# Row maxima over 256 and 512 keys instead of 384 and 384, with a mask copy, a sign step and two sums in other places

## The chip, the cores and the metric

The kernel runs on one core of one Trainium2 chip. The metric is the device time of one execution in microseconds (us). Five engines work side by side, each through its own queue in order: TensorE (PE, matrix products), VectorE (DVE), ScalarE (ACT), GpSimd (POOL) and SyncE (SP, which issues most DMAs). They wait for each other through semaphores. A matrix product reads its operands from the on-chip memory SBUF and leaves its result in PSUM, of which the tiles named `wide`, `sc` and `turned` are parts.

## What is computed

Routing attention and then a feed-forward layer with a gate. Cut to what matters:

```python
# q, k, v: (4, 8, 768, 64); centroids: (8, 16, 64)
q_assign = argmax(q_n . c_n); k_assign = argmax(k_n . c_n)     # nearest of 16 clusters
mask = q_assign[..., :, None] == k_assign[..., None, :]
scores = where(mask, (q @ k.T) / 8, -1e9)
scores = scores - max(scores, axis=-1)
attn = exp(scores); attn = attn / (sum(attn) + 1e-9)
x = attn @ v                                                   # then (3072, 512)
h = x @ w_in                                                   # (3072, 2048)
out = (h * erf(softplus(h))) @ w_out                           # (3072, 512)
```

## The kernel before

The kernel has an attention stage of about 400 us and a feed-forward stage of about 550 us. The diff touches the first.

A *pair* is two heads of one batch entry; there are 16 pairs (0 to 15), each with its two heads in rows 0 to 63 and 64 to 127. A pair is worked in 12 *units*: `units[u]` is a pair, a half of its 768 queries (384) and a block of 128 keys. Two units make a *period*, so `period(p, i)` with i from 0 to 5 is called 96 times, and i = 0, 1, 2 belong to the first half of the queries and i = 3, 4, 5 to the second. All instructions are kept in the order in which the program writes them, per engine: the wrapper `InOrder` records them, which is why nearly every row of the profile has its line, L131.

A row's maximum must be known before its exponentials. So half a pair ahead, `maxima_step` computes a bound on the scores of one block of 128 queries in bfloat16: two passes of matrix products into `wide` (`qv` times `kv`, the values; `qm` times `km`, the cluster masks), one product for each head, and then a DVE reduction of `wide` into `nmx`. There is one `wide`. A block's 768 keys are taken in two such steps of 384 keys, so a period has two: the *first step* (`step_ahead(u)`) with both passes on 64 rows, and the *second step* (`step_ahead(u + 1, True)`), which is a generator: its first pass stands alone, and its second pass uses only rows 32 to 63 and 96 to 127, beside the score products on rows 0 to 31 and 64 to 95. With every third block (periods 2 and 5) a small reduction into `lowest` follows, and `turn` brings the bounds into a row of `qm` in the next period.

In a period PE does, in this order: in periods 0 and 3 `turn`; the first step; `products` of units u and u + 1 (float32, into two `sc` buffers that are reused every two units); the first pass of the second step; `scores(u)` with the second pass of the second step beside it; `scores(u + 1)`; in some periods a product for a mask of the next pair, into `turned`; in period 3 `similarities` of the pair after the next one; `attend` for the two units before (float32, into `turned`); and in periods 0 and 3 the first product of `divide`, which sums the denominators.

DVE's queue has the two reductions, and between them: in periods 1 and 4 the three operations of `divide` (`den`, two on `turned`, one into `more_out`); the cluster choice of `choose`, in period 3 as `sims`, a maximum that is stored in a corner of the `sc` buffer of unit u + 1, and `hot`, in period 5 `aside`, in period 0 `hotT`; transposes of q and k; and, in period 0, one mask copy into `km` (`masks`, with `copied_by` set to DVE).

ACT has the exponentials (`curve(u)`, `curve(u + 1)`) that read `sc` and write one of eight tiles `pr`, the logarithm and exponential of `divide`, and the other mask copies.

POOL sums the exponentials: `accumulate` adds each unit's `pr` to a running sum in `more_out`. Its first sum of each half takes the first two units at once, in periods 1 and 4.

Beside this, in pairs 1 to 11, 22 of the 32 blocks of the feed-forward weights are converted, two blocks a pair. A block (`n`) goes through `size` and `rest` (ACT), `bounded` and `shifted` (DVE, each 128x512 from SBUF to SBUF, the first float32 and the second uint32), `sign` (ACT, from 128x512 to int16) and `summed` (POOL, which needs `sign` and `shifted`), after which SP issues the `fetch` of the block five later. For one block of a pair, `n1 - 1`, `bounded`, `shifted` and `sign` are in period 0 and `summed` in period 1; for the other, `n1`, `bounded`, `sign` and `shifted` are in period 3 and `summed` in period 4. In pairs 12 to 15 (`FORMS`) some sums of the weights take the place.

Of the kernel before, what the change touches and what calls it, by code (L numbers as in the profile page):

```python
# [14 lines left out]
ALU = mybir.AluOpType  # L15
ACT = mybir.ActivationFunctionType
AX = mybir.AxisListType
PSUM = bass.MemoryType.PSUM

P = 128  # L20
B, H, S, D = 4, 8, 768, 64
C = 16
NJ = S // P
# [15 lines left out]

UP = 2.0**16  # L40
PLACES = 5
FORMS = {12: {0: 1}, 13: {0: 1}, 14: {0: 1, 3: 1}, 15: {0: 1, 3: 2, 4: 2, 5: 2}}
POOL_FORMS = range(12, 16)
BIG = 2.0**60
# [95 lines left out]
def kernel(  # L140
# [178 lines left out]
    def sign(n):  # L319
        hi, _, upper = steps[n]  # L320
        turned_sign = n < 4 * DM // P and n // (DM // P) % 2 == 0
        ae.activation(
            out=upper, in_=hi, func=ACT.Prelu, scale=-(2.0**-25) if turned_sign else 2.0**-25, alpha=2.0**90
        )
# [78 lines left out]
    def choose(p, spare=None, aside=False):  # L403

        if p >= NPAIR:
            return
        st = pairs[p]
        n = HW // C
        sims = routep.tile([P, HW], F32, name="sims")
        ve.transpose(out=sims, in_=st.pop("psim"))  # L410
        yield
        sim = sims.rearrange("p (g c) -> p g c", c=C)
        mx = (wide[:, 0] if spare is None else spare)[:, 512 - n :]
        ve.reduce_max(out=mx, in_=sim, axis=AX.X)
        yield
        hot = routep.tile([P, HW], BF16, name="hot")
        ve.tensor_tensor(
            out=hot.rearrange("p (g c) -> p g c", c=C), in0=sim,
            in1=mx.unsqueeze(2).to_broadcast([P, n, C]), op=ALU.is_equal,
        )  # L420
        yield
        if aside:
            st["aside"] = routep.tile([P, HW], BF16, name="aside")
            ve.transpose(out=st["aside"][D + Q :], in_=hot[D : D + Q])
            yield
        st["hotT"] = routep.tile([P, HW], BF16, name="hotT")
        ve.transpose(out=st["hotT"], in_=hot)
# [5 lines left out]
    def masks(p, nm, half, bank, narrow=False, copied_by=ae):  # L433

        if p >= NPAIR:
            return lambda: None
        st = pairs[p]
        cols = slice(half * HW, (half + 1) * HW)
        r, hot = slice(0, D) if nm == "q" else slice(D, P), st["hotT"]
        picked = pick[r, half]  # L440
        if narrow:
            r = slice(r.start + Q, r.stop)
            picked = pick[r, 1]
            hot = hot if half else st["aside"]
        won = bank[:, 0:HW]
        te.matmul(won, lhsT=picked, rhs=hot[r], start=True, stop=True)
        if nm == "q":
            return lambda: ae.activation(out=st["qm"][:, cols], in_=won, func=ACT.Relu)
        if copied_by is ve:
            return lambda: ve.tensor_scalar(  # L450
                out=st["km"][:, cols], in0=won, scalar1=BIG, scalar2=nbig, op0=ALU.mult, op1=ALU.add
            )
        return lambda: ae.activation(
            out=st["km"][:, cols], in_=won, func=ACT.Identity, bias=nbig, scale=BIG
        )

    turns = []

    def maxima_step(p, i, sm=wide, behind=False):

        st = pairs[p]
        nmx = maxima[p % 2]
        t, half = divmod(i, 2)

        def passes(a, b, start, rows):
            for e in range(2):
                r = slice(e * D + rows.start, e * D + rows.stop)
                te.matmul(
                    sm[:, e, 0:HW], lhsT=st[a][r, t * P : (t + 1) * P],
                    rhs=st[b][r, half * HW : (half + 1) * HW], start=start, stop=not start,  # L470
                )

        passes("qv", "kv", True, slice(0, D))
        if behind:
            yield
        passes("qm", "km", False, slice(Q, D) if behind else slice(0, D))
        if behind:
            yield
        ve.tensor_reduce(
            out=nmx[:, :, t, half], in_=sm[:, :, 0:HW], axis=AX.X, op=ALU.max, negate=True  # L480
        )
        if i in (NJ - 1, 2 * NJ - 1):
            h = i // NJ
            ve.tensor_reduce(
                out=lowest[h][:, :, ::D].rearrange("p t e -> p e t"),
                in_=nmx[:, :, h * HJ : (h + 1) * HJ], axis=AX.X, op=ALU.min,
            )
            turns.append((p, h))
# [48 lines left out]
    def curve(u):  # L537

        pr = prs[u % NPT]
        sc = sc_of.pop(u)[:, :, 0:HW].rearrange("p e (c x) -> p e c x", c=2)  # L540
        ae.activation(out=pr[:, :, :, 0:QW], in_=sc, func=ACT.Exp, scale=D**-0.5)
# [801 lines left out]

    def step_ahead(u, behind=False):
        p, i = divmod(u + NJ, 2 * NJ)
        steps = maxima_step(p, i, behind=behind) if p < NPAIR else iter(())
        if not behind:
            run(steps)
        return steps
# [7 lines left out]
    def period(p, i):  # L1357
        u = 2 * NJ * p + 2 * i
        n1, n2 = 2 * p - 1, 2 * p
        early = lambda n: 0 <= n < N_EARLY  # L1360

        def mask(place):
            which = (MASKS if p else FIRST_MASKS).get((i, place))
            if which:
                return masks(p + 1, *which, turned[0 if i in (0, 5) else 1], place > 1, ve if i == 0 else ae)
            return lambda: None

        if u > 0:
            for which in turns if i in (0, 3) else ():
                turn(*which)  # L1370
                turns.remove(which)
            step_ahead(u)
        mask(0)()
        next(part[0], None)
        if i == 5:
            next(routing[0], None)
        if i == 0 and p:
            run(routing[0])
        if u == 2:
            next(routing[0])  # L1380
        products(u)
        products(u + 1)
        mask(1)()
        second = step_ahead(u + 1, True) if u > 0 else iter(())
        next(second, None)
        rows = D if u == 0 or u + NJ >= len(units) else Q
        scores(u, rows)
        next(second, None)
        if i:
            next(second, None)  # L1390
        next(part[0], None)
        scores(u + 1, rows)
        later = mask(2)
        if i == 0:
            later()
            later = lambda: None
            next(second, None)
        if i == 3:
            similarities(p + 2)
            routing[0] = choose(p + 2, sc_of[u + 1][:, 0], True)  # L1400
        curve(u)
        later()
        curve(u + 1)
        if u == 0:
            step_ahead(1)
            similarities(1)
            routing[0] = choose(1, turned[0])
            next(routing[0])
            next(routing[0])
            vectors(1, "q")  # L1410
            vectors(1, "k")
        if i == 0 and early(n1 - 1):
            bounded(n1 - 1)
            shifted(n1 - 1)
            sign(n1 - 1)
        elif i == 1 and early(n1):
            size_and_rest(n1)
        elif i == 3 and early(n1):
            bounded(n1)
            sign(n1)  # L1420
        elif i == 5 and early(n2):
            rest(n2)
        for _ in range(min(len(forms), FORMS.get(p, {}).get(i, 0))):
            forms.pop(0)[0]()
        if i == 3:
            next(routing[0], None)
            if early(n1):
                shifted(n1)
            for _ in range(2):
                next(routing[0], None)  # L1430
        elif i == 1:
            load(p + 1, "v", v, vp)
            if p == 0:
                run(routing[0])
                transposes(2, "q")
        elif i == 2:
            transposes(p + 2, "k")
        elif i == 4:
            vectors(p + 2, "k")
            vectors(p + 2, "q")  # L1440
        elif i == 5:
            transposes(p + 3, "q")
        if u > 0:
            if i == 1 and early(n1 - 1):
                summed(n1 - 1)
            elif i == 4 and early(n1):
                summed(n1)
            for w in (u - 2, u - 1):
                accumulate(w)
            if i % HJ == 1 and p in POOL_FORMS and forms:  # L1450
                forms.pop(0)[1]()
            for w in (u - 2, u - 1):
                attend(w)
            if i % HJ == 0:
                part[0] = divide(u - 1)
                next(part[0])
        if i == 3 and early(n2):
            size(n2)

# [185 lines left out]
```

## Time and profile before

| | |
|---|---|
| median of 3 runs | 964.01 us (963.83 to 964.29) |
| the profiled execution | 963.98 us |
| its span, from the first instruction to the last | 962.2 us |
| mean granted clock of TensorE | 1.00 |

The costliest groups of the attention stage, from the fifth part of the page (line, engine, operation, output and inputs with partitions x elements, count, then busy time in all and mean ns of one, then the engine's idle time ahead of them):

```profile
L131 POOL TENSOR_TENSOR more_out<-more_out,pr 128x768 f32<-128x768 f32 x128 | 217.1, 1696 | 18.5 <-ACT pr L131 10.0
L131 DVE TENSOR_REDUCE nmx<-wide 128x2 f32<-128x768 f32 x189 | 180.5, 955 | 47.8 <-PE wide L131 47.0
L131 ACT ACTIVATE pr<-sc 128x768 f32<-128x768 f32 x192 | 148.7, 810 | 94.3 <-PE wide L131 78.7
L131 PE MATMUL turned<-pr,in_v 128*32 128x193 f32 x3072 | 144.8, 330 | 0.0
```

A timeline row has the start and the length in us from the span's start, the engine, the operation, its output and inputs, the shapes, how many of them follow each other, and in brackets how long the engine was idle before and what ended that. A length is from the start of the first to the end of the last of the row; on DVE and ACT an operation is shown to begin up to a tenth of a us or more before the one ahead of it has ended, and on PE several products run at once. A row of windows has, for each stretch, its length and the busy time of PE, weight loads, DVE, ACT and POOL with the number of instructions, then the granted clock, the DMA share and GB/s. A row of the chain of waits has a start, a length and what the end waited for in that time.

### The profile page before, as it was taken

The page shows a single profiled execution, that of the slowest core. Times are in us where ns is not written, and L with a number is a line of the kernel's source. Part 1 is how long each engine was busy: PE and PEld are TensorE (multiplying, and loading weights), DVE is VectorE, ACT ScalarE, POOL GpSimd, SP SyncE. Part 2 cuts the span into 40 slices and gives each one's busy share as a digit, 9 for nine tenths or more (in the row PEclk, how much of TensorE's full clock was granted, in tenths as well). Part 3 has the DMA queues.
Part 4 walks back from the last instruction along what each step waited for, and adds up shares of the span by engine and source line. Part 5 has one row for each costly group of instructions (what it writes and reads, how often), then busy time and mean ns, then how long its engine had stood idle before and what let it go on. Part 6 is the DMA issues. An engine that isn't in the chain of part 4 may idle for free.

```text
span 962.2 us, 22508 instructions
## 1 busy us (share of the span) xinstructions
PE 953.1 (99%) x8954; PEld 729.3 (76%) x8954; DVE 772.0 (80%) x1336; ACT 550.2 (57%) x839; POOL 544.7 (57%) x385
## 2 busy tenths in 40 slices
PE   8999999999999999999999999999999999999998
PEld 3555555555555555588888888998999899889987
DVE  8888888888888887878879878488847966795787
ACT  3777777777777665557624442564258226724651
POOL 1688888778787888835789902650353054206500
PEclk9999999999999999999999999999999999999999
DMA  9444444446444311282994349653564538254423
GB/s 214 83 112 111 111 111 109 107 110 174 89 111 111 68 35 35 67 276 66 182 206 192 144 168 233 215 183 118 189 201 129 166 135 260 75 186 156 152 88 110
DMA packets 180921, 134.42 MB, mean 140 GB/s; under 512 B 131888, under 2 KB 141616, under 8 KB 180784
## 3 DMA queue, kind: packets, MB, share of 16 engines
q1 hardware_dynamic: 173600, 123.37, 44.2%
q0 software_dynamic: 4720, 9.18, 5.4%
q8 instruction: 71, 1.16, 0.5%
q10 hardware_dynamic: 2496, 0.43, 0.2%
q14 instruction: 34, 0.28, 0.1%
HBM read 99.39 MB, written 35.39 MB: 140 GB/s over the span
## 4 chain that ended last, share of the span: by engine, by line
PE 95%; DVE 2%; POOL 1%; DMA 1%; issue 1%; ACT 0%; SPq 0%; DVEq 0%; POOLq 0%; ACTq 0%
PE bank L131 42%; PE turned L131 31%; PE sc L131 16%; PE wide L131 6%; POOL more_out L131 1%; DVE nmx L131 1%; DMA g_more<-in_moe_w_out_dram 0%; DMA in_q<-in_q_dram 0%; DVE kT L131 0%; DVE turned L131 0%; DVE sims L131 0%; POOL x_more L131 0%; DVE qT L131 0%; DVE more_out L131 0%; ACT pr L131 0%
## 5 line engine op out<-in xcount | busy, mean ns | idle before, releaser
L131 POOL TENSOR_TENSOR more_out<-more_out,pr 128x768 f32<-128x768 f32 x128 | 217.1, 1696 | 18.5 <-ACT pr L131 10.0
L131 DVE TENSOR_REDUCE nmx<-wide 128x2 f32<-128x768 f32 x189 | 180.5, 955 | 47.8 <-PE wide L131 47.0
L131 ACT ACTIVATE pr<-sc 128x768 f32<-128x768 f32 x192 | 148.7, 810 | 94.3 <-PE wide L131 78.7
L131 PE MATMUL turned<-pr,in_v 128*32 128x193 f32 x3072 | 144.8, 330 | 0.0
L131 PEld LDWEIGHTS turned<-pr,in_v 128*32 128x32 f32 x3072 | 91.5, 109 | 50.7 <-issue 21.3
L131 DVE TENSOR_TENSOR g<-g,bank 128x512 f32<-128x512 f32 (+1 forms) x139 | 77.9, 578 | 50.1 <-PE bank L131 44.2
L131 PE MATMUL bank<-x_own,w_in 128*128 128x128 f32 (+1 forms) x712 | 106.6, 296 | 0.0
L131 POOL TENSOR_TENSOR x_own<-x_own 128x512 f32<-128x512 f32 x16 | 23.0, 1448 | 146.7 <-DVE x_own L131 133.9
L131 PE MATMUL sc<-qT,kT 64*128 64x384 f32 x528 | 98.3, 486 | 0.0
L131 PEld LDWEIGHTS bank<-x_own,w_in 128*128 128x128 f32 x712 | 94.2, 192 | 4.7 <-DVE g L131 0.8
L131 DVE TENSOR_TENSOR g<-g 128x512 f32<-128x512 f32 x114 | 79.0, 693 | 20.0 <-PE bank L131 14.2
L131 POOL TENSOR_TENSOR g<-g,osb 128x512 f32<-128x512 f32 x40 | 51.9, 1310 | 48.5 <-DVE g L131 35.5
L131 PE MATMUL bank<-w_out,g 128*128 128x256 f32 x336 | 77.0, 379 | 0.0
L131 POOL TENSOR_TENSOR more_out<-pr,pr 128x768 f32<-128x768 f32 x32 | 60.4, 1887 | 28.3 <-ACT pr L131 28.3
L131 PEld LDWEIGHTS bank<-w_out,g 128*128 128x128 f32 x336 | 63.7, 190 | 9.0 <-DVE g L131 0.3
L131 PE MATMUL bank<-g_more,g 128*128 128x256 f32 x288 | 68.3, 380 | 0.0
L131 PEld LDWEIGHTS <-qv 64*128 64x128 bf16 x384 | 27.0, 93 | 53.0 <-issue 36.9
L131 PEld LDWEIGHTS sc<-qT,kT 64*128 64x128 f32 x528 | 50.0, 187 | 21.3 <-ACT inv L131 2.4
L131 PE MATMUL wide<-kv,qv 64*128 64x384 bf16 x378 | 64.1, 328 | 1.3 <-DVE nmx L131 0.6
L131 PE MATMUL wide<-km,qm 64*128 64x384 bf16 (+1 forms) x378 | 62.6, 327 | 0.0
L131 DVE TENSOR_TENSOR g<-a_s,g 128x512 f32<-128x512 f32 x64 | 59.8, 971 | 3.1 <-ACT a_s L131 3.1
L131 ACT ACT_TABLE_LOAD x40 | 51.3, 1283 | 18.5 <-DVE g L131 17.9
(215 smaller groups left out, 1994.8 us busy)
## 6 DMA issues: line engine op xcount, KB each, us to landing
g_more<-b_dram SPq DMA_DIRECT2D x48, 512.0 KB, 3.3
w_in<-a_dram SPq DMA_DIRECT2D x64, 256.0 KB, 3.4
more_in<-a_dram SPq DMA_DIRECT2D x48, 256.0 KB, 3.5
x_own<-in_moe_w_in_dram SPq DMA_DIRECT2D x13, 512.0 KB, 4.4
in_v<-in_v_dram SPq DMA_DIRECT2D x32, 192.0 KB, 3.0
x_dram<-more_out SPq DMA_DIRECT2D x128, 48.0 KB, 1.8
x_own<-x_dram SPq DMA_DIRECT2D x6, 1024.0 KB, 5.9
in_k<-in_k_dram SPq DMA_DIRECT2D x59, 96.0 KB, 2.7
```

Of the source, the lines that this page charges most:

```text
L131: ins = getattr(self.engine, name)(*args, **kw)
```

## The change

Four edits, and what moves with them:

1. `maxima_step` takes `cut`, the key at which the two steps divide. From unit 12 on (pair 1), in periods 0, 1, 3 and 4, the first step takes 256 keys and the second 512. In periods 2 and 5, and before unit 12, it stays 384 and 384.
2. The mask copy of period 0 moves from DVE to ACT, for all pairs that have it (the masks of pairs 2 to 15, in pairs 1 to 14), and it stands behind the second step's reduction in the program and ahead of `curve(u)` on ACT. The moved `later()` changes nothing in other periods.
3. `sign(n1 - 1)` of period 0 moves behind the first product, the logarithm and the exponential of `divide`.
4. `accumulate` of the two units before now stands ahead of `summed`, in period 1 and in period 4.
5. With `summed` moves the `fetch` behind it; nothing else changes its order.

```diff
+NARROW = 2 * P
...
-    def maxima_step(p, i, sm=wide, behind=False):
+    def maxima_step(p, i, sm=wide, behind=False, cut=HW):
...
+        keys = slice(cut, S) if half else slice(0, cut)
+        width = keys.stop - keys.start
...
-                    sm[:, e, 0:HW], lhsT=st[a][r, t * P : (t + 1) * P],
-                    rhs=st[b][r, half * HW : (half + 1) * HW], start=start, stop=not start,
+                    sm[:, e, 0:width], lhsT=st[a][r, t * P : (t + 1) * P],
+                    rhs=st[b][r, keys], start=start, stop=not start,
...
-            out=nmx[:, :, t, half], in_=sm[:, :, 0:HW], axis=AX.X, op=ALU.max, negate=True
+            out=nmx[:, :, t, half], in_=sm[:, :, 0:width], axis=AX.X, op=ALU.max, negate=True
...
     def step_ahead(u, behind=False):
         p, i = divmod(u + NJ, 2 * NJ)
-        steps = maxima_step(p, i, behind=behind) if p < NPAIR else iter(())
+        cut = NARROW if u >= 2 * NJ and u // 2 % HJ < HJ - 1 else HW
+        steps = maxima_step(p, i, behind=behind, cut=cut) if p < NPAIR else iter(())
...
-                return masks(p + 1, *which, turned[0 if i in (0, 5) else 1], place > 1, ve if i == 0 else ae)
+                return masks(p + 1, *which, turned[0 if i in (0, 5) else 1], place > 1)
...
         later = mask(2)
         if i == 0:
-            later()
-            later = lambda: None
             next(second, None)
         if i == 3:
             similarities(p + 2)
             routing[0] = choose(p + 2, sc_of[u + 1][:, 0], True)
+        if i == 0:
+            later()
+            later = lambda: None
         curve(u)
         later()
         curve(u + 1)
...
         if i == 0 and early(n1 - 1):
             bounded(n1 - 1)
             shifted(n1 - 1)
-            sign(n1 - 1)
...
         if u > 0:
+            for w in (u - 2, u - 1):
+                accumulate(w)
             if i == 1 and early(n1 - 1):
                 summed(n1 - 1)
             elif i == 4 and early(n1):
                 summed(n1)
-            for w in (u - 2, u - 1):
-                accumulate(w)
...
             if i % HJ == 0:
                 part[0] = divide(u - 1)
                 next(part[0])
+        if i == 0 and early(n1 - 1):
+            sign(n1 - 1)
```

## The prediction

> **What bounds the kernel now.** I read the first and fourth parts of the page, then the attention stage pair by pair, since the diff touches nothing else.
>
> ```profile
> span 962.2 us, 22508 instructions
> PE 953.1 (99%) x8954; PEld 729.3 (76%) x8954; DVE 772.0 (80%) x1336; ACT 550.2 (57%) x839; POOL 544.7 (57%) x385
> PE 95%; DVE 2%; POOL 1%; DMA 1%; issue 1%; ACT 0%; SPq 0%; DVEq 0%; POOLq 0%; ACTq 0%
> ```
>
> TensorE (PE) is busy 99% of the span and is 95% of the chain that ended last, so time moves only with PE's own work or with a new hole in it. Six consecutive periods (pair 7, from 190.10 us) are one turn of the loop:
>
> ```profile
> 202.14:206.80 4.66, 4.66 (x70) 2.47 (x70) 3.81 (x7) 3.48 (x6) 3.17 (x2) 1.00 0.52 84
> sum 24.44, PE 24.44 PEld 13.90 DVE 21.02 ACT 19.15 POOL 19.63; mean PE 4.07 PEld 2.32 DVE 3.50 ACT 3.19 POOL 3.27
> ```
>
> In these windows PE fills all 24.44 us of a pair at granted clock 1.00, with VectorE (DVE) 21.02 behind it. The chain of waits shows where DVE already touches PE:
>
> ```profile
> 195.98 0.19 PE wide L131 x2
> 203.86 0.16 PE wide L131 x2
> 208.61 0.20 PE wide L131 x2
> ```
>
> These are the first pass of the second maxima step in periods 1, 3 and 4. It must wait until DVE has reduced the first step out of the same tile `wide`. Period 3 does not wait (0.16). Periods 1 and 4 pay 0.03 and 0.04, of which I count 0.02 for period 1. So there DVE is already exactly as late as PE can bear.
>
> **The narrow and wide steps on PE.**
>
> ```profile
> 210.62 0.34 PE L131 MATMUL wide<-kv,qv 64*128 64x384 bf16 x2
> 210.79 0.33 PE L131 MATMUL wide<-km,qm 64*128 64x384 bf16 x2
> 210.95 1.45 PE L131 MATMUL sc<-qT,kT 64*128 64x384 f32 x8
> ```
>
> From start to start a pass over 384 keys takes 0.17 and 0.16 us; 128 keys are 0.053. The first step has two passes with nothing beside them: 256 keys save 0.107, of which I count 0.10, since the next weights must load meanwhile. The second step's first pass is alone too: 512 keys add 0.053. Its second pass uses 32-row strips that the score matmuls leave free. Whether the longer strip holds up the other strips, this view answers:
>
> ```profile
> 320.65 0.32 PE L131 MATMUL turned<-hotT,pick 64*128 64x384 bf16 x1
> 320.65 1.61 PE L131 MATMUL sc<-qT,kT 64*128 64x384 f32 x8
> ```
>
> The mask copy occupies rows 0 to 63 from 320.65; a score matmul starts on the other rows at the same 320.65 and the two halves then run staggered. Row strips run on their own, so I take 0 for that pass (bounds: 0, and 0.053 if strips march together), but in period 0 the narrow mask matmul stands behind it in its strip: 0.05. PE's balance is -0.05 in periods 1, 3 and 4, and 0 in period 0. Pairs 1 to 14 have all four narrow periods, pair 15 periods 0 (without mask) and 1.
>
> **DVE: same total, other places.** Reductions go from two of 768 numbers to 512 and 1024. Between 768 numbers (0.96) and 384 (0.55, below) lies 1.07 ns a number, so the first is 0.27 shorter and the second 0.27 longer. This is the queue of period 3:
>
> ```profile
> 204.40 0.96 DVE L131 TENSOR_REDUCE nmx<-wide 128x2 f32<-128x768 f32 x1 [0.83 <-PE wide L131]
> 204.41 1.51 ACT L131 ACTIVATE pr<-sc 128x768 f32<-128x768 f32 x2 [1.15 <-PE wide L131]
> 205.27 0.42 DVE L131 TENSOR_SCALAR w_in<-w_in 128x512 f32<-128x512 f32 x1
> 205.60 0.58 DVE L131 STREAM_TRANSPOSE sims<-turned 128x384 f32<-128x384 f32 x1
> 206.10 0.39 DVE L131 TENSOR_SCALAR w_in<-w_in 128x512 uint32<-128x512 uint32 x1
> 206.41 0.55 DVE L131 TENSOR_REDUCE sc<-sims 128x24 f32<-128x384 f32 x1
> 206.99 0.55 DVE L131 TENSOR_TENSOR hot<-sims,sc 128x384 bf16<-128x384 f32 x1
> 207.46 0.95 DVE L131 TENSOR_REDUCE nmx<-wide 128x2 f32<-128x768 f32 x1
> 208.47 0.34 PE L131 MATMUL wide<-kv,qv 64*128 64x384 bf16 x2
> 207.26 1.29 POOL L131 TENSOR_TENSOR w_in<-w_in,x_own 128x512 int32<-128x512 int32 x1 [1.87 <-ACT x_own L131]
> 208.51 1.85 POOL L131 TENSOR_TENSOR more_out<-pr,pr 128x768 f32<-128x768 f32 x1
> ```
>
> DVE runs without a hole from 204.40 to period 4's first reduction. Its start is bound to the end of period 3's second step: -0.10 +0.05 +0.05 on PE, so unmoved. The 0.27 added at its head and saved at its tail cancel. So in pairs 1 to 11 PE's savings of periods 3 and 4 are swallowed at period 4's second step, whatever else happens, and only its 0.05 longer pass remains.
>
> **The order on GpSimd (POOL), the term that decides.** Look at POOL above: it sits idle 1.87 us, until the sign step on ScalarE (ACT) ends, with `summed` at the head of its queue. In that hole lie both DVE operations on `w_in` (`bounded`, 205.27; `shifted`, 206.10). The edit puts the accumulations ahead of `summed` in periods 1 and 4, so POOL no longer waits for the sign but only for the two exponentials. The first accumulation's start then shows in pair 12, which has no `summed`:
>
> ```profile
> 326.75 1.51 ACT L131 ACTIVATE pr<-sc 128x768 f32<-128x768 f32 x2 [1.15 <-PE wide L131]
> 328.34 1.83 POOL L131 TENSOR_TENSOR more_out<-pr,pr 128x768 f32<-128x768 f32 x1 [1.14 <-ACT pr L131]
> 328.40 0.56 DVE L131 TENSOR_REDUCE sc<-sims 128x24 f32<-128x384 f32 x1
> ```
>
> It starts 0.08 after the exponentials end and lasts 1.83. In pair 7 that is 204.41 + 1.51 + 0.08 = 206.00, to 207.83. `shifted` would start at 206.10 + 0.27 = 206.37, inside it. What POOL does to such an operation stands in the stage after the attention:
>
> ```profile
> 441.04 1.28 POOL L131 TENSOR_TENSOR more_out<-more_out,w_out 128x512 f32<-128x512 f32 x1
> 441.31 1.30 DVE L131 TENSOR_SCALAR w_out<-w_out 128x512 f32<-128x512 f32 x1 [0.86 <-ACT w_out L131]
> 442.28 1.48 POOL L131 TENSOR_TENSOR w_out<-w_out,g_more 128x512 int32<-128x512 int32 x1
> 443.38 0.67 DVE L131 TENSOR_SCALAR w_out<-w_out 128x512 uint32<-128x512 uint32 x1
> ```
>
> These are the same two operations on other weights. Alone they take 0.42 and 0.39; begun inside a POOL operation they end 0.29 after it (442.61 after 442.32; 444.05 after 443.76). The reduction at 328.40, inside the accumulation, keeps its 0.56. So `shifted` ends at 207.83 + 0.29 = 208.12 instead of 206.49.
>
> What is late next: the reduction behind it and `hot` end 1.05 later, at 209.17 (before 207.54). `hot` reads the score bank that period 4's second pair of score matmuls needs, and these take 0.65 (the eight at 210.95 last 1.45, less 0.16 by which the last outlives its place, halved). A signal from DVE to PE takes 0.06 (207.46 + 0.95 to 208.47), so PE reaches its second step at 209.17 + 0.06 + 0.65 = 209.88. The other condition, the short reduction, ends at 209.17 - 0.08 + 0.68 = 209.77 and releases PE at 209.83, a little earlier. Before, that step started at 208.47. The hole is 1.41; the exponentials may come 0.05 sooner, since period 3's scores start 0.05 sooner, so I take 1.38. `bounded` (205.54 to 205.96) is just out in time. POOL then has `summed` waiting for `shifted`, and everything in the pair moves back together.
>
> The Trainium skill, "SBUF — State Buffer", section "Who interferes with whom", says that DVE and GpSimd share a port pair, that a `tensor_scalar` in a two-port mode takes it, and that whoever issues first keeps it for its whole instruction. The four rows above agree that the DVE waits. If the waiting operation then needed its whole 0.39 instead of 0.29, as that rule reads, each pair would cost 0.10 more and the sum would be 979.5.
>
> **Edits that cost nothing, and their cover.**
>
> ```profile
> 192.45 1.51 ACT L131 ACTIVATE pr<-sc 128x768 f32<-128x768 f32 x2 [0.67 <-PE sc L131]
> 192.63 0.62 DVE L131 TENSOR_SCALAR km<-turned,nbig 128x384 bf16<-128x384 f32 x1 [0.55 <-PE turned L131]
> 193.17 0.95 DVE L131 TENSOR_REDUCE nmx<-wide 128x2 f32<-128x768 f32 x1
> 194.03 0.88 DVE L131 TENSOR_SCALAR w_in<-w_in 128x512 f32<-128x512 f32 x2
> 193.84 1.35 ACT L131 ACTIVATE x_own<-x_own 128x512 int16<-128x512 f32 x1
> 194.92 0.43 ACT L131 ACTIVATE inv<-turned,alleps 128x192 f32<-128x192 f32 x1
> 196.53 1.51 PE L131 MATMUL turned<-pr,in_v 128*32 128x193 f32 x32
> 201.16 0.57 ACT L131 ACTIVATE km<-turned,nbig 128x384 bf16<-128x384 f32 x1
> ```
>
> Mask copy: without it DVE reduces from about 192.42 instead of 193.17, which removes period 1's 0.02 although this reduction is 0.27 longer. On ACT the copy (0.57) starts about 192.63 and moves the exponentials' end from 193.96 to about 194.6; their reader starts at 196.53, so 1.9 us cover it. Without that cover it would cost up to 0.57 x 14 = 8 us. Sign: 1.35 behind the division's two operations; these start at about 194.55 instead of 194.92, the sign some 0.8 later, and ACT is free again 1.08 after that (as from 193.84 to 194.92), at 196.4, just before the scores that its next exponentials read are done (196.53, when PE turns to the next work). By the same working `summed` ends about 1.4 later in period 1 (behind the sign) and 0.9 in period 4 (behind `shifted`), and with it the next weight fetch on SP; behind that fetch stand only stores of x and loads for a later pair. Without `summed` ahead of it the accumulation chain has more air than before. In period 0 nothing of the kind happens: `bounded` and `shifted` would run from 193.55 to 194.43, and the accumulation starts at 194.6 + 0.08.
>
> **The sum.** Pairs 1 to 11: +1.38 (hole), +0.05 (wider pass of period 4), -0.07 (period 1), 0 (period 0): +1.36, times 11 = +15.0. Pairs 12 to 14 have neither `bounded` nor `shifted`: 3 x 3 x -0.05 = -0.45. Pair 15: -0.10. Together +14.4 on the profiled execution's 963.98 (span 962.2 and 1.8 around it), 978.4; the median, 964.01, is 0.03 from it. The stages behind only start later.
>
> Bounds: if the blocked operation ended with POOL's, without the 0.29, the hole would be 1.09 and the time about 975. POOL's first accumulation reached 2.35 beside a DVE operation,
>
> ```profile
> 316.41 2.35 POOL L131 TENSOR_TENSOR more_out<-pr,pr 128x768 f32<-128x768 f32 x1 [1.08 <-ACT pr L131]
> ```
>
> which would add 0.52 x 11 = 5.7 (984); marching strips add 0.05 in 44 periods, 2.3 us (987 with both).
>
> **The rivals.** 1. `shifted` is not blocked here (not slower). Then `hot` is 0.27 later only, PE reaches period 4's second step 0.04 later, a pair costs 0.04 + 0.05 - 0.07, and the sum is 0.2 - 0.55: 963.7. For it: the two operations keep 0.42 and 0.39 today. Against: today they lie in POOL's hole of 1.87. It decides if `shifted` starts before POOL, 0.37 us away.
> 2. The PE saving arrives whole: 14 x 3 x 0.053 + 0.1 + 11 x 0.04 = 2.8, so 961.2. Against: DVE's unbroken queue in period 3.
> 3. Period 0 is caught too. Its accumulation would have to start 0.7 sooner than worked out; then `shifted` ends at 196.8, the next second step waits 1.8, and 11 pairs add 19: 997.
>
> **How the numbers follow.** Forecast 0.80, rival 1 0.08, rival 2 0.05, rival 3 0.07. The range 973 to 987 is the forecast with its bounds and leaves out the three rivals. This kernel's measurement can tell 0.2% (1.9 us) from no change: faster 0.05, same 0.08, slower 0.87.
>
> **What would show it.** In pairs 1 to 11 a uint32 operation on `w_in` of about 1.7 us in period 3, ending 0.29 after a POOL accumulation that began before it; a hole of 1.4 in PE within period 4's scores; none in pair 12; pairs of about 25.8 us up to the eleventh and no longer than now after it. The forecast is wrong if that operation keeps 0.39, or if it is long and PE has no hole.

## The result, and the profile after

| | before | after |
|---|---|---|
| median | 963.92 us (963.36 to 964.29, 6 runs) | 979.81 us (979.51 to 980.17, 6 runs) |
| ratio after / before, 95% interval | | 1.0166 [1.0152, 1.0179] |
| profiled execution; its span | 963.98; 962.2 us | 979.83; 978.1 us |

The changed kernel is slower by 15.9 us, and the span has grown by the same 15.9. Of the page of the kernel after, the span, the busy time of each engine and the chain by engine:

```profile
span 978.1 us, 22508 instructions
PE 954.9 (98%) x8954; PEld 722.5 (74%) x8954; DVE 779.5 (80%) x1322; ACT 561.1 (57%) x853; POOL 543.8 (56%) x385
PE 92%; DVE 3%; ACT 1%; issue 1%; POOL 1%; DMA 1%; SPq 0%; DVEq 0%; ACTq 0%; POOLq 0%
```

The instruction count is the same, 14 operations went from DVE to ACT, and PE is shown busy for 1.8 us more than before (953.1). So about 14 of the 15.9 us are time in which PE stands still. The windows of periods 3 and 4 of pair 7 say where (length, busy PE, weight loads, DVE, ACT, POOL):

```profile
211.10:216.04 4.94, 4.88 (x72) 2.39 (x70) 3.79 (x6) 3.81 (x6) 3.76 (x3) 1.00 0.50 83
216.04:221.25 5.21, 3.97 (x56) 1.98 (x53) 5.14 (x9) 2.90 (x7) 2.55 (x3) 1.00 0.32 94
```

Period 4 lasts 5.21 us and PE works 3.97 of them. Before, its window of 3.80 us was all busy. The granted clock is 1.00 in both. The timeline of the same stretch, with what the prediction said would be there:

```profile
213.38 1.23 DVE L132 TENSOR_REDUCE nmx<-wide 128x2 f32<-128x1024 f32 x1 [1.15 <-PE wide L132]
213.39 1.51 ACT L132 ACTIVATE pr<-sc 128x768 f32<-128x768 f32 x2 [1.10 <-PE wide L132]
...
214.85 0.58 DVE L132 STREAM_TRANSPOSE sims<-turned 128x384 f32<-128x384 f32 x1
214.98 1.84 POOL L132 TENSOR_TENSOR more_out<-pr,pr 128x768 f32<-128x768 f32 x1 [1.10 <-DMA in_k<-in_k_dram]
215.35 1.76 DVE L132 TENSOR_SCALAR w_in<-w_in 128x512 uint32<-128x512 uint32 x1
215.57 0.53 PE L132 MATMUL turned<-more_out,minus 128*32 128x192 f32 x8
217.03 0.55 DVE L132 TENSOR_REDUCE sc<-sims 128x24 f32<-128x384 f32 x1
217.61 0.55 DVE L132 TENSOR_TENSOR hot<-sims,sc 128x384 bf16<-128x384 f32 x1
218.09 0.68 DVE L132 TENSOR_REDUCE nmx<-wide 128x2 f32<-128x512 f32 x1
218.31 0.92 PE L132 MATMUL sc<-qT,kT 64*128 64x384 f32 x4 [1.24 <-DVE hot L132]
219.03 0.41 PE L132 MATMUL wide<-kv,qv 64*128 64x512 bf16 x2
```

POOL's accumulation starts 0.08 after the exponentials end (213.39 + 1.51) and runs to 216.82. (The row names a load of k as what ended POOL's wait, other pairs name `bounded`. Both merely ended close by: the start is 0.08 behind the exponentials in all eleven pairs, and also in run 4 below, where `bounded` ends 0.24 ahead of them.) `shifted` begins inside it at 215.35, takes 1.76 instead of 0.39 and ends 0.29 behind it. `hot` then ends at 218.16, the score products that need its bank start at 218.31, and PE has stood 1.24 us. In pairs 1 to 11 that is once a pair, and the list of waits sums it to PE's largest:

```profile
PE sc L132 <- DVE hot L132: 13.5, 11, 1.2
```

The chain of waits over the same place shows how it can mislead:

```profile
216.16 0.43 ACT inv L132
...
216.61 0.37 ACT inv L132
...
217.03 0.56 DVE sc L132
...
217.61 0.56 DVE hot L132
```

It puts 0.80 us on the division's two ACT operations. But the maximum at 217.03 reads only `sims`, and the corner of `sc` that it writes was free once the exponentials were through at 214.90; it starts when DVE's queue is free of `shifted` (217.11 less the overlap with which DVE's rows are shown), and an ACT operation merely ended close by. Nothing on ACT was late, as the first and third runs below show.

### The profile page after: what moved, and what is told of

The parts are those of the page before. It is cut to its first block, busy times and chain, and to the rows that moved or that the text cites. A ratio compares the mean times of both kernels' runs of the same rounds, so it can differ in the third digit from the quotient of the medians.

```text
span 978.1 us, 22508 instructions
## 1 busy us (share of the span) xinstructions
PE 954.9 (98%) x8954; PEld 722.5 (74%) x8954; DVE 779.5 (80%) x1322; ACT 561.1 (57%) x853; POOL 543.8 (56%) x385
## 4 chain that ended last, share of the span: by engine, by line
PE 92%; DVE 3%; ACT 1%; issue 1%; POOL 1%; DMA 1%; SPq 0%; DVEq 0%; ACTq 0%; POOLq 0%
PE bank L132 41%; PE turned L132 31%; PE sc L132 15%; PE wide L132 5%; POOL more_out L132 1%; DVE nmx L132 1%; ACT inv L132 1%; DVE hot L132 1%; DVE sc L132 1%; DMA g_more<-in_moe_w_out_dram 0%; DMA in_q<-in_q_dram 0%; DVE kT L132 0%; ACT pr L132 0%; DVE sims L132 0%; DVE turned L132 0%
## 5 line engine op out<-in xcount | busy, mean ns | idle before, releaser
L132 DVE TENSOR_REDUCE nmx<-wide 128x2 f32<-128x512 f32 (+2 forms) x189 | 180.6, 956 | 64.0 <-PE wide L132 62.9
L132 PEld LDWEIGHTS sc<-qT,kT 64*128 64x128 f32 x528 | 47.9, 187 | 29.6 <-ACT w_in L132 9.1
L132 PE MATMUL wide<-kv,qv 64*128 64x256 bf16 (+2 forms) x378 | 64.2, 328 | 1.1 <-ACT km L132 0.6
L132 PE MATMUL wide<-km,qm 64*128 64x256 bf16 (+3 forms) x378 | 62.6, 327 | 0.0
L132 PEld LDWEIGHTS bank<-g_more,g 128*128 128x128 f32 x288 | 54.5, 190 | 8.1 <-issue 0.8
```

What stands on the lines that cost most here:

```text
L132: ins = getattr(self.engine, name)(*args, **kw)
```

## The experiments

Lengths of the periods, from the start of one first step to the next, in a typical pair among 2 to 11 (period 5 is 3.92 in all of them). A few single periods are longer, for a reason that no run here settles: period 0 of pairs 6 and 9 by 0.33 and 0.18 in the kernel before, period 2 of pair 1 by 0.32 in the changed one. Times are medians; the ratios are to the kernel before on the same chip, whose median was 963.8 to 963.9 each time.

| kernel | us | ratio [95%] | period 1 | 2 | 3 | 4 | 0 |
|---|---|---|---|---|---|---|---|
| before | 963.92 | | 3.79 | 4.09 | 4.73 | 3.82 | 4.09 |
| after | 979.81 | 1.0166 [1.0152, 1.0179] | 3.71 | 4.09 | 4.94 | 5.20 | 4.09 |
| 1. sums first in period 4 | 964.65 | 1.0009 [1.0000, 1.0018] | 3.71 | 4.09 | 4.94 | 3.84 | 4.09 |
| 2. accumulations first, alone | 998.02 | 1.0356 [1.0336, 1.0377] | 5.28 | 4.09 | 4.73 | 5.46 | 4.09 |
| 3. `shifted` behind `hot` | 965.54 | 1.0018 [1.0009, 1.0028] | 3.71 | 4.09 | 4.94 | 3.92 | 4.09 |
| 4. no narrow steps | 981.22 | 1.0182 [1.0165, 1.0199] | 3.76 | 4.09 | 4.73 | 5.46 | 4.09 |
| 5. narrow steps alone | 972.25 | 1.0087 [1.0073, 1.0100] | 3.71 | 4.17 | 4.94 | 3.84 | 4.30 |
| 6. mask copy back on DVE | 986.48 | 1.0233 [1.0217, 1.0249] | 5.00 | 4.20 | 4.94 | 3.84 | 4.30 |
| 7. `sims` first | 966.14 | 1.0024 [1.0014, 1.0033] | 3.71 | 4.09 | 4.68 | 4.23 | 4.09 |
| 8. narrow in two periods | 962.24 | 0.9985 [0.9976, 0.9994] | 3.71 | 4.09 | 4.73 | 3.83 | 4.09 |
| 9. the same, `shifted` last | 962.21 | 0.9983 [0.9974, 0.9991] | 3.71 | 4.09 | 4.73 | 3.83 | 4.09 |
| 10. the same, interleaved | 961.82 | 0.9978 [0.9969, 0.9987] | 3.71 | 4.09 | 4.73 | 3.81 | 4.09 |
| 11. the same, `hot` ahead of `shifted` | 960.92 | 0.9969 [0.9957, 0.9981] | 3.71 | 4.09 | 4.73 | 3.71 | 4.09 |

**1. The order of period 4 alone undone.**

```diff
+            if i == 4 and early(n1):
+                summed(n1)
             for w in (u - 2, u - 1):
                 accumulate(w)
...
-            elif i == 4 and early(n1):
-                summed(n1)
```

> The changed kernel with `summed` ahead of the accumulations again in period 4 (period 1 stays changed). Theory (the first accumulation blocks `shifted`): `shifted` keeps 0.39 in period 3, the hole of 1.24 on TensorE in period 4 goes. What stays in pairs 1 to 11 is `hot` 0.27 later by the longer reduction, with a dearer restart about +0.2 at period 4's second step, +0.05 for its longer pass, -0.08 in period 1: (0.17 x 11) - 0.55 = +1.3, so 965.3 us, between 963.5 and 966.5. Rival A (the longer second reduction in DVE's queue makes the hole): about 980, as the changed kernel.

Measured: 964.65 us. In its timeline (pair 7) POOL waits for the sign again, and `shifted` is short:

```profile
206.87 0.38 DVE L132 TENSOR_SCALAR w_in<-w_in 128x512 uint32<-128x512 uint32 x1
207.75 1.29 POOL L132 TENSOR_TENSOR w_in<-w_in,x_own 128x512 int32<-128x512 int32 x1 [2.35 <-ACT x_own L132]
207.76 0.55 DVE L132 TENSOR_TENSOR hot<-sims,sc 128x384 bf16<-128x384 f32 x1
...
209.18 0.41 PE L132 MATMUL wide<-kv,qv 64*128 64x512 bf16 x2
```

POOL's idle time comes back (2.35 us here) and 15.2 of the 15.9 us go. The order in this one period is the cause; what the other edits leave is 0.15 a pair in pairs 1 to 11.

**2. That edit alone, on the kernel before.**

```diff
 # on the kernel before
+            for w in (u - 2, u - 1):
+                accumulate(w)
             if i == 1 and early(n1 - 1):
                 summed(n1 - 1)
             elif i == 4 and early(n1):
                 summed(n1)
-            for w in (u - 2, u - 1):
-                accumulate(w)
```

> The kernel before with nothing but the accumulations ahead of `summed` in periods 1 and 4 (384 keys everywhere, mask copy on DVE, sign ahead of the division). Theory: in period 4 about +1.57 in pairs 1 to 11, as in the changed kernel or a little more; and in period 0 the exponentials end 193.96 in pair 7, the first accumulation starts 194.04, `shifted` wants to start at 194.48 and ends at 196.16 instead of 194.91, so period 1's second step is 1.25 later: 11 x 2.8 = +31, about 995 us. If only period 4 is hit: 981. Rival A (the longer reduction): 964, no change. Rival B (any reordering on GpSimd is harmless): 964 or less.

Measured: 998.02 us, 3 us above what was expected. Period 0 is caught too, as the timeline of pair 7 shows:

```profile
212.68 2.38 DVE L131 TENSOR_SCALAR w_in<-w_in 128x512 f32<-128x512 f32 x2
212.69 2.09 POOL L131 TENSOR_TENSOR more_out<-pr,pr 128x768 f32<-128x768 f32 x1 [1.14 <-ACT pr L131]
215.98 0.34 PE L131 MATMUL wide<-kv,qv 64*128 64x384 bf16 x2 [1.35 <-DVE nmx L131]
```

`bounded` comes 0.01 ahead of POOL, keeps its 0.42, and POOL's accumulation takes 2.09 instead of 1.82. `shifted` follows inside it and ends 0.28 behind it, so that the two DVE operations take 2.38 instead of 0.88. The 0.27 by which the accumulation grew is what the expectation lacked: period 1 is 1.50 longer instead of 1.25. Only in pair 6, where DVE is late in period 0, does POOL come first and `bounded` itself is caught. Period 4 is 1.64 longer: 3.14 x 11 = 34.5 against 34.2 measured. This is the third rival's mechanism of the prediction, met where edits 2 and 3 are missing.

**3. The late operation moved, POOL's order left.**

```diff
-            next(routing[0], None)
+            for _ in range(3):
+                next(routing[0], None)
             if early(n1):
                 shifted(n1)
-            for _ in range(2):
-                next(routing[0], None)
```

> The changed kernel with `shifted` of period 3 behind `hot` instead of between `sims` and the maximum; GpSimd's order is the changed one. Theory: `shifted` is still caught by the accumulation, but starts at 3.14 after the second step's reduction began and ends 0.29 after the accumulation, at 3.70, so that its row shows about 0.55 to 0.6; `hot` is in time, and period 4's second step waits for the first reduction until about 4.36 instead of 4.07: 11 x (0.29 + 0.05 - 0.08) - 0.55 = +2.3, 966.3 us, between 965 and 968. Rival C (the accumulation slows everything on DVE, not this one operation): 975 or more, the maximum and `hot` longer than 0.56.

Measured: 965.54 us. POOL is as early as in the changed kernel:

```profile
207.22 1.83 POOL L132 TENSOR_TENSOR more_out<-pr,pr 128x768 f32<-128x768 f32 x1 [1.10 <-DMA in_k<-in_k_dram]
208.37 0.55 DVE L132 TENSOR_TENSOR hot<-sims,sc 128x384 bf16<-128x384 f32 x1
208.84 0.50 DVE L132 TENSOR_SCALAR w_in<-w_in 128x512 uint32<-128x512 uint32 x1
```

The maximum and `hot` run beside POOL at their usual lengths. `shifted` meets only the last 0.21 us of the accumulation, and ends 0.29 behind it as ever. What still stands behind it is the reduction of period 4's first step: it ends at 209.94, PE's second step starts 0.06 later, and period 4 is 3.92 instead of the 3.84 of run 1. So it was the blocked operation's place ahead of `hot`, not POOL's early start as such.

**4. All but the narrow steps.**

```diff
-        cut = NARROW if u >= 2 * NJ and u // 2 % HJ < HJ - 1 else HW
+        cut = HW
```

> The changed kernel with 384 and 384 keys in every period (edits 2 to 4 alone: mask copy, sign, accumulations first). Theory: `shifted` starts 0.27 sooner but ends where the accumulation lets it, 0.29 behind it, so the hole in period 4 is the same or larger by what the narrow step saved: about +1.55 in pairs 1 to 11, -0.03 in period 1, nothing in pairs 12 to 15: +16.7, 980.7 us. Rival A (the longer reduction makes the hole): 964.

Measured: 981.22 us. `shifted` (215.77, 2.03 us) ends at 217.80, 0.28 behind POOL's 217.52, and period 4 is 5.46. The steps of 256 and 512 keys have no part in the loss; with them the kernel is 1.4 us faster. Here PE's second step waits for period 4's first reduction, with them for the products behind `hot`, which let it start 0.06 sooner, counted from period 3's second reduction; the rest is 0.05 a pair in period 1 and what pairs 12 to 15 gain.

**5. The narrow steps alone.**

```diff
 # on the kernel before
-        steps = maxima_step(p, i, behind=behind) if p < NPAIR else iter(())
+        cut = 2 * P if u >= 2 * NJ and u // 2 % HJ < HJ - 1 else HW
+        steps = maxima_step(p, i, behind=behind, cut=cut) if p < NPAIR else iter(())
 # and maxima_step as in the change
```

> The kernel before with the steps of 256 and 512 keys alone; mask copy, sign and accumulations stay where they were. Theory: nothing is blocked on DVE, so period 4 has no hole of 1.4, and periods 3 and 4 together are 0.23 longer, as they were where `summed` stood ahead in period 4. Period 1 gives back its saving, since period 0's reduction is 0.27 longer behind a mask copy that is still on DVE: 3.78 to 3.84 instead of 3.71. Together 0.23 to 0.28 a pair more, times 11, less 0.5: 966 to 967 us. Rival E (mask copy and sign have no part in it): period 1 at 3.71 and 964.65 us, as with `summed` ahead. Rival F (the steps themselves bring the 15 us): 979.

Measured: 972.25 us, 5 us above what was expected. Periods 3 and 4 came as expected, and period 1 kept its saving, as rival E had it (the time is far from rival E's). Two things had been missed. In period 0 the longer reduction stands behind the mask copy and ends so late that the next first step, which writes the same `wide`, waits for it; the chain of waits:

```profile
195.84 1.14 DVE nmx L131
...
197.03 0.39 PE wide L131 x4
```

That costs 0.21. The division on DVE ends later by it and holds the mask product of period 2, which writes `turned`, by 0.08. And in pairs 12 to 14, where no `shifted` is left, a sum of the weights on DVE is caught in period 0. Its rows of pair 12, first before, then here:

```profile
316.40 0.68 DVE L131 TENSOR_TENSOR more_in<-w_in 128x512 f32<-128x512 f32 x1
316.41 2.35 POOL L131 TENSOR_TENSOR more_out<-pr,pr 128x768 f32<-128x768 f32 x1 [1.08 <-ACT pr L131]
```

```profile
321.02 1.81 POOL L131 TENSOR_TENSOR more_out<-pr,pr 128x768 f32<-128x768 f32 x1 [1.10 <-ACT pr L131]
321.30 2.08 DVE L131 TENSOR_TENSOR more_in<-w_in 128x512 f32<-128x512 f32 x1
```

Before, DVE came first by 0.01 us and POOL paid, where it had the time. With the reduction 0.27 longer POOL comes first and DVE pays 1.40, which makes period 1 of these pairs 4.80 instead of 3.76. The Trainium skill, "SBUF — State Buffer", section "Who interferes with whom", says that an operation of two SBUF inputs meets GpSimd's reads as well, and that the order of issue decides who waits. Both rows bear it out. A pair among 1 to 11 is 0.45 longer and one of pairs 12 to 14 1.27; pair 15 is 0.10 shorter. Together 0.45 x 11 + 1.27 x 3 - 0.10 = 8.7, for the 8.45 measured.

**6. The mask copy of period 0 back on DVE** (the order of period 4 as in 1).

```diff
-                return masks(p + 1, *which, turned[0 if i in (0, 5) else 1], place > 1)
+                return masks(p + 1, *which, turned[0 if i in (0, 5) else 1], place > 1, ve if i == 0 else ae)
...
         if i == 0:
+            later()
+            later = lambda: None
             next(second, None)
...
-        if i == 0:
-            later()
-            later = lambda: None
```

> The changed kernel with `summed` ahead in period 4 and the mask copy of period 0 back on DVE, ahead of the second reduction; the sign step stays behind the division. Theory: this edit is what keeps period 0 clear in the changed kernel. With the copy back, the exponentials end 0.5 sooner and so does POOL's accumulation, which stands ahead of `summed` in period 1, and `bounded` comes some 0.5 later: it begins inside the accumulation and ends 0.28 behind it. Period 1's second step then waits for its reduction: 5.0 to 5.1 instead of 3.71; and period 0 is 0.21 longer as where the steps alone were changed (4.30). In pairs 12 to 14 the DVE operation on `more_in` is caught in its place, 1.1 and 0.2 a pair. 11 x 1.57 + 3.9 more than 964.65: 986 us, 982 to 989. Rival I (the place of the sign step keeps period 0 clear, and the mask copy matters for its own time alone): period 1 at 3.71 and 967 to 969 us.

Measured: 986.48 us, as worked out. Period 0 is caught in pairs 1 to 14 (from pair 12 on it is the sum of the weights, as in run 5). Pair 7:

```profile
204.25 1.82 POOL L132 TENSOR_TENSOR more_out<-pr,pr 128x768 f32<-128x768 f32 x1 [1.09 <-ACT pr L132]
204.53 2.28 DVE L132 TENSOR_SCALAR w_in<-w_in 128x512 f32<-128x512 f32 x2
207.47 0.39 PE L132 MATMUL wide<-kv,qv 64*128 64x512 bf16 x2 [1.11 <-DVE nmx L132]
```

So the mask copy's move is worth 22 us in the presence of the other edits. Its own 0.6 us on DVE are little of that. Counted from the start of period 0, `bounded` comes 0.74 earlier by the move (3.42 instead of 4.16) and POOL's accumulation 0.60 later (4.49 instead of 3.89), and so the two operations are out of POOL's way. The sign step was behind the division in this run as well, so its place alone does not keep period 0 clear; whether it is needed beside the mask copy's move was not tried.

**7. `sims` ahead of `bounded`** (the rest as in 1), for the 0.2 by which period 3 is longer.

```diff
-        elif i == 3 and early(n1):
-            bounded(n1)
-            sign(n1)
...
             next(routing[0], None)
             if early(n1):
+                bounded(n1)
+                sign(n1)
                 shifted(n1)
```

> The changed kernel with `summed` ahead in period 4 and, in period 3, `bounded` and the sign step behind the transposition `sims` instead of ahead of it. Period 3 had 4.94 instead of 4.73 us there. Theory: its denominators' product waits for `sims`, which reads the bank that it writes; with `sims` 0.4 earlier that wait goes and period 3 falls to 4.68 to 4.73, while `hot` ends where it did, so period 4 grows by what period 3 lost, to about 4.05, and the time stays at 964.65 within 0.7. Rival G (the 0.2 come from the longer pass itself, not from `sims`): period 3 stays at 4.94 and period 4 at 3.84. Rival H (the sign step, now 0.4 to 0.6 later, makes `summed` and the accumulations behind it late for period 5's denominators): period 5 over 3.92 and the time above 966.

Measured: 966.14 us. Period 3 falls from 4.94 to 4.68 as expected: the denominators' product does wait for `sims`, which reads the bank that it writes (after: `sims` ends at 215.43, the product starts at 215.57). Period 4 grew by 0.39 instead of 0.26, so the total missed the band. `hot` ends 0.13 later. The likely reason is that `shifted` now follows `bounded`, whose result it reads, with nothing between: the two start 0.41 apart, where `bounded` and `sims` had started 0.33 apart.

**8 to 11. A version that beats both.** Period 3 gains nothing from a longer second reduction, for DVE has no air there. So the narrow steps stay only where they paid, on top of experiment 1:

```diff
-        cut = NARROW if u >= 2 * NJ and u // 2 % HJ < HJ - 1 else HW
+        cut = NARROW if u >= 2 * NJ and u // 2 % NJ in ((1, 4) if u < 24 * NJ else (0, 1, 3, 4)) else HW
```

> The changed kernel with `summed` ahead of the accumulations in period 4, and with steps of 256 and 512 keys only in periods 1 and 4 up to pair 11, in periods 0, 1, 3 and 4 from pair 12 on. Theory: where the second reduction of period 3 keeps 768 numbers, nothing in DVE's queue is longer than before, so neither `sims` nor `hot` comes later, and the narrow first step saves what it saved in pairs 12 to 14: period 1 at 3.71 instead of 3.79, period 4 at 3.71 to 3.75 instead of 3.82, period 3 at 4.73 as before. That is 0.15 to 0.19 a pair, times 11, and 0.55 in pairs 12 to 15: 961.3 to 961.8 us, a gain of about 0.25%. Rival D (DVE is just in time whatever the steps are, so the narrow step in period 4 only moves PE's wait to `hot`): period 4 stays at 3.82 and the time is 962.5 or more.

Measured: 962.24 us. Period 1 gave its 0.08; period 4 stayed at 3.83, as rival D had it (its time of 962.5 was undercut a little): `hot` ends at 206.68 and the second step starts 0.87 later, at 207.55.

In run 9 `shifted` moves behind `hot`, as in 3.

> As with the steps of 256 and 512 keys in two periods and `summed` ahead in period 4 (962.24 us), and `shifted` behind `hot` in period 3. There period 4 still had 3.83 us instead of the 3.71 of pair 12, and PE's second pair of score products started as `hot` ended. Theory: `hot` is what is late; 0.39 sooner it is out of the way, `shifted` is not blocked since `summed`, ahead of the accumulations, waits for it, and the reduction of period 4's first step ends where it ended, in time. Period 4 falls to 3.71 to 3.75, 0.08 to 0.12 a pair, times 11: 960.8 to 961.4 us, 0.3% under the kernel before. Rival J (the reduction of the first step, still behind all of DVE's queue, is as late as `hot`): period 4 stays at 3.83 and the time at 962.2.

Measured: 962.21 us, rival J. `hot` was no longer late, but the reduction of period 4's first step was. It ended 3.99 behind the start of period 3's second reduction instead of 3.75:

```profile
204.71 0.58 DVE L132 STREAM_TRANSPOSE sims<-turned 128x384 f32<-128x384 f32 x1
205.40 0.56 DVE L132 TENSOR_REDUCE sc<-sims 128x24 f32<-128x384 f32 x1
206.80 0.69 DVE L132 TENSOR_REDUCE nmx<-wide 128x2 f32<-128x512 f32 x1
207.54 0.39 PE L132 MATMUL wide<-kv,qv 64*128 64x512 bf16 x2
```

The maximum starts 0.69 behind `sims`, which it reads. In experiment 1, `shifted` started 0.50 behind `sims` and the maximum 0.30 behind that, so an operation placed there had cost 0.11, not 0.39. Run 10 uses both such places: `sims`, `bounded`, maximum, `shifted`, `hot`.

> As with steps of 256 and 512 keys in two periods and `summed` ahead in period 4 (962.24 us); in period 3 `bounded` and the sign step now stand between `sims` and the reduction that reads it, and `shifted` between that reduction and `hot`. With `shifted` behind `hot` DVE took 2.42 us from the start of `bounded` to that of period 4's first reduction, with `shifted` between `sims` and its reader 2.19: an operation that reads what the one ahead of it writes starts 0.15 to 0.2 later than another would. Theory: with an independent operation behind both `sims` and the reduction, the five take 2.19 less 0.15 = 2.04; `hot` and the reduction of the first step both end 0.15 sooner, so neither is late, and period 4 falls from 3.83 to 3.71: 960.9 us, 960.5 to 961.4. Rival K (the gap behind a dependent operation is only shown, not spent; DVE's total stays): period 4 at 3.83 and 962.2. Rival L (the sign step, 0.5 later, makes POOL late): periods 4 or 5 above 3.85 and 3.93 and the time above 962.6.

Measured: 961.82 us, short of the theory. DVE's five took 2.06, nearly as worked out, so the gap is spent and rival K fails by its mechanism, but `sims` starts 0.98 behind the second reduction, where `bounded` had started at 0.88, so that `hot` gained only 0.02. Run 11 puts `shifted` behind `hot` again and keeps `bounded` between. Its code in period 3, in place of `bounded` and the sign step ahead of `sims` and of `shifted` behind it:

```python
             next(routing[0], None)
             if early(n1):
                 bounded(n1)
                 sign(n1)
             for _ in range(2):
                 next(routing[0], None)
             if early(n1):
                 shifted(n1)
```

> As where `bounded` and `shifted` were interleaved (961.82 us, period 4 at 3.81, since `hot` ended only 0.02 sooner in its period), with `shifted` behind `hot`: `sims`, `bounded`, the reduction, `hot`, `shifted`. From the spacings of the runs before (0.98 to `sims`, then 0.50, 0.31, 0.58, 0.47, 0.34) `hot` begins 2.37 behind the second reduction of period 3 instead of 2.58, and period 4's first reduction 3.18 instead of 3.04, so that it ends 3.87 behind; PE, not held up, would come to the second step 3.92 behind. Theory: both are then just in time, period 4 falls to 3.71 to 3.75, 11 x 0.06 to 0.10 less: 960.7 to 961.2 us. Rival M (the reduction is late again, as with `shifted` behind `hot` before): period 4 at 3.80 or more and 961.7 or more.

Measured: 960.92 us (960.47 to 961.38), a ratio of 0.9969 [0.9957, 0.9981] to the kernel before: 3.0 us faster. Its period 4:

```profile
203.18 0.96 DVE L132 TENSOR_REDUCE nmx<-wide 128x2 f32<-128x768 f32 x1 [0.83 <-PE wide L132]
205.55 0.55 DVE L132 TENSOR_TENSOR hot<-sims,sc 128x384 bf16<-128x384 f32 x1
206.35 0.69 DVE L132 TENSOR_REDUCE nmx<-wide 128x2 f32<-128x512 f32 x1
207.10 0.38 PE L132 MATMUL wide<-kv,qv 64*128 64x512 bf16 x2
```

`hot` begins 2.37 and the reduction 3.17 behind 203.18, as worked out, and period 4 is 3.71, as it also is in pairs 12 to 14. The order of run 11 with steps of 384 keys was not tried, so what each of the two is worth alone is open.

## Why the prediction was right, and what it mis-sized

- **What bounds, and that PE's saving is swallowed.** Right. PE's first passes fell to 0.12 and 0.11 apart, and pairs 12 to 14 gained 0.05 in each of periods 1, 3 and 4, and pair 15 0.05 in each of periods 0 and 1, as forecast.
- **The order on POOL.** Right, and shown from both sides: undone, the loss goes (1); done alone, it comes (2); with the caught operation out of the way, POOL's early start is harmless (3). The first rival (not blocked) falls with the row at 215.35, the second (the whole saving) with experiment 1, which without any block is still no faster than before. The third (period 0 caught) shows in no row here; where it did come, in run 2, it cost 1.50 a pair instead of 1.8.
- **The remnant of 0.29.** The caught operation ended 0.28 to 0.29 behind POOL in runs 2, 3 and 4 and in the changed kernel, whether it had met 1.5 us of it or 0.2. As the prediction reads the Trainium skill, "SBUF — State Buffer", section "Who interferes with whom", its whole 0.39 would follow. That reading, 979.5, lies nearer to the time, but only because another term was too small.
- **What `hot`'s delay costs, the mis-sized term.** "a signal from DVE to PE takes 0.06" and "these take 0.65" made 0.71 from `hot`'s end to the second step. Measured are 0.87 (218.16 to 219.03), and 0.87 again in experiment 1 (208.31 to 209.18), in runs 8 and 10 and, within 0.01, in 7. The 0.06 is that of the passes over `wide`. Here 0.15 go by from `hot`'s end to the first product (0.14 from `sims` to the denominators' product), and the four products take 0.72. That is 0.16 too little in each of eleven pairs, 1.8 us. With it the sum is 980.2 for the 979.83 of the profiled run; the longer single periods named above, 0.51 before and 0.32 after, make 0.2 of what is left. When `hot` comes was right: the prediction puts it 1.63 later (its "1.05 later" counts from the end of `shifted`), and it came 1.64 later behind period 3's second reduction. In the kernel before this path ended at 207.54 + 0.87 = 208.41, just ahead of the 208.47 at which the second step starts, so no row there showed its true length.
- **Period 3.** Forecast 0.05 shorter, it became 0.21 longer, by the wait for `sims`. That was not foreseen. It changed nothing in the sum, since PE stood for `hot` later in any case: experiment 7 took that wait away and the time did not fall. It is also why PE's idle row is 1.24 and not the 1.4 of the forecast: period 3 had already spent a part.
- **Period 0 and the free edits.** Right. The timeline of the kernel after:

```profile
202.63 0.88 DVE L132 TENSOR_SCALAR w_in<-w_in 128x512 f32<-128x512 f32 x2
203.70 1.82 POOL L132 TENSOR_TENSOR more_out<-pr,pr 128x768 f32<-128x768 f32 x1 [1.69 <-ACT pr L132]
```

  Both DVE operations are through 0.19 before POOL starts. Experiment 6 shows that this cover is the mask copy's move. The prediction works the order out (194.43 against 194.68), but names the mask copy for the time that it moves, and not for this order, on which 22 us hang.
- **The range.** Its upper end is the forecast with both bounds that cost time. For its lower end, 973, the prediction gives no working; its own low bound was 975.

## What to carry to other kernels

Where two engines can lock each other out, an order of instructions that only "waits less" on one of them may start it inside the other's urgent work: work out who comes first, and put behind the urgent operation what can be caught. An idle stretch of an engine off the path, here POOL's 1.87 us, can be the reason why its neighbour is undisturbed. Before spending a saving on one engine, look whether the next engine's queue has any air in that same period; here, up to pair 11, a saving on PE was worth having in two periods of six, in one of them only after DVE's queue had been put in another order, and worthless in a third.

## What the runs showed of the hardware beyond that

- A caught `tensor_scalar` of 0.38 to 0.42 us ends 0.28 to 0.29 us after POOL's operation, whether it came 0.1 or 1.6 us into it (runs 2, 3 and 4), and the `tensor_tensor` of 0.68 us (128x512, two inputs) 0.55 after it (run 5). About 0.11 to 0.13 us of each seem to have passed already; why is not settled.
- Two DVE operations of which one reads the other's result start 0.58 and 0.69 apart (lengths 0.55 and 0.58), with an independent one behind the first 0.46 and 0.50. Such a gap can be filled: moving a 0.38 us operation into it made the kernel of run 11 1.3 us faster than run 9, which has it ahead of `sims`.
- PE starts 0.05 to 0.06 us after a DVE operation ends when the waiting product is a bfloat16 pass over `wide`, and 0.14 to 0.15 after it when it is a float32 product. In the changed kernel the weights of the late product are shown to load only right ahead of it (from 218.28 for a product at 218.31); whether that is the whole difference was not tried.
